# The first inverse stage on quarters of the array: symmetric halves instead of 49 full outputs, unfolded on VectorE

## The chip, the cores and the metric

The kernel runs on one core of one Trainium2 chip. The metric is the device time of one execution in microseconds (us), as the median of several runs. An execution is also profiled; the profile names the engines PE (TensorE products, PEld its weight loads), DVE (VectorE), ACT (ScalarE), POOL (GpSimd) and SP (SyncE, which here issues nearly all the DMAs).

## The reference

Two blocks over x of shape (8, 3136, 256): a frequency-domain block, then a Fourier mixing block with an MLP.

```
X  = rfft(x, axis=1);  Y = soft_threshold(X @ complex weights + bias, 0.01)
y  = irfft(Y, n=3136, axis=1)                  # block 1
u  = y + real(fft(fft(y, axis=1), axis=2))     # block 2
un = (u - mean(u)) / sqrt(var(u) + 1e-6)       # over the 256 columns
out = u + relu(un @ w_ch1) @ w_ch2             # 256 -> 1024 -> 256
```

All of it is float32. 3136 = 64 x 49, so a position is n = 49 n1 + n2 with n1 below 64 and n2 below 49, and a transform along the sequence is done in two stages.

## The kernel before

The eight sequences go through one after the other, in overlapping phases: the forward transform (p1, p2_f2), the products with the complex weights (p2_w), the mixing values (p2_mix), the inverse transform (p2_yt, p2_g2 and the start of p3_norm) and the MLP (p3_tr, p3_mlp1, p3_mlp2). Each phase of each sequence is a generator that yields a due time; the program resumes the earliest one, and what it then writes goes into the engines' queues. T is the due time of one sequence, some 215 us in the middle of the run. Each engine works its queue in order, so the code's due times set what stands behind what.

The frequencies of a sequence lie in 32 slots u of up to 50 values; a quarter q of the work holds 8 slots. The inverse transform has two stages.

- First stage, per slot: `p2_yt` transposes the spectrum Y (tile `y`) on PE into `g_yt`, two slots and 512 columns at a time (L908), and takes it out of PSUM. `p2_g2` multiplies it with a table `tif` (100 frequencies by 98 outputs: 49 values of n2 times two parts) into `g_g` (named g_g2 in the program), and DVE copies that to `bev` (L941), which goes to DRAM as `bd`. Sequence 0 does this in plain float32 with one product (L937). Sequences 1 to 7 split both operands into a high and a low fp32r part (ACT casts `yh`, `tih`, L919 and L900; DVE subtracts for `yl`, `til`, L157) and run three fp32r products through `mm3` (L163, L164, L165). Four steps i per quarter, two slots each: 16 steps per sequence.
- Second stage: `p3_norm` loads four pairs of n2 rows from `bd` as `bf` (`load_bf`, L974), multiplies them with `inv_f` over the slots, and DVE adds the mixing values `mt` (L1061). The products run on quarters of the array: `quads` cuts the 128 x 128 array into four 64 x 64 pieces with an operand each, `pair` takes two PSUM banks and has DVE clear one column of each as a mark (L370), and `run_quads` issues the products one behind the other (first L378, then L383). Six groups of 8 rows each per sequence, and a seventh for the last sequence that collects what is left over of all eight.

PSUM: all these tiles (`g_...`) rotate through the four banks of tag g; `h` and `o` of the MLP have two banks each. In the MLP, PE makes `h`, ACT and DVE turn it into `hh` and `hl` (L1109, L1110), and PE reads those for `o`.

The same cut into quarters is used by the second forward stage (`g_f<-tff,af`), and from sequence 3 on by the first one (`g_f<-xf,fwd_f`), where DVE first replaces the two halves of `xf` by sum and difference (L521, L522); each of those runs is put right behind a second-stage run of the inverse (`waiting`).

Of the kernel before, what the change touches and what calls it, by code (L numbers as in the profile page):

```python
# [55 lines left out]
def tables():  # L56
# [23 lines left out]
    for u in range(U):  # L80
# [14 lines left out]
        else:  # L95
# [8 lines left out]
            ti[1, :z, u, 1] = (co * sg).T / N  # L104
    p = np.arange(128)
# [10 lines left out]
        ti=ti.transpose(0, 1, 2, 4, 3).reshape(100, U, 98),  # L116
        cs=cs, mask=mask, ident=np.eye(128),
# [23 lines left out]
def spectral_block(ctx: ExitStack, tc: tile.TileContext, x, w_ri, b_ri, w1, w2,  # L141
                   c_fwd, c_fwd0, c_inv, c_tf, c_ti, c_cs, c_mask, c_ident, out):
# [69 lines left out]
    inv_f = cp.tile([128, 128], F32, name="inv_f")  # L212
    nc.sync.dma_start(out=fwd_0, in_=c_fwd0)
# [79 lines left out]
    lows = [cp.tile([100, 2, 128], F32, name=f"low{i}") for i in range(2)]  # L293
    for t in lows:
        va.memset(t[:, :, 0:1], 0.0)
# [40 lines left out]

    def n2_rows(t, n0, n):

        return t[n0:n0 + n].rearrange("n c u d -> (c u) n d")
# [367 lines left out]
    def p2_w(b):  # L707

        for q in range(4):
# [5 lines left out]
            y = sb.tile([128, 2, 8, 2, S], F32, tag="Y", bufs=2, name="Y")  # L715
# [58 lines left out]
    def p2_mix(b):  # L774
# [12 lines left out]
        for q in range(4):  # L787
# [4 lines left out]
            if b == 0:  # L792
                ef = sb.tile([128, 2, 8, S], F32, tag=("eh", "el")[q % 2], bufs=1, name="ef")
            else:
                eh = sb.tile([128, 2, 4, 100], F32R, tag="eh", bufs=1, name="eh")
                el = sb.tile([128, 2, 4, 100], F32R, tag="el", bufs=1, name="el")
# [78 lines left out]
    def p2_yt(b):  # L875

        for q in range(4):
# [6 lines left out]
            for i in range(4):  # L884
                yield base + STEP * (M0 + 0.022 + 0.185 * i)
                s = i // 2
                if i % 2 == 0:
                    if b == 1 and q == s == 0:
                        tif = tabs.pop((1, 0))
                    else:  # L890
                        tag = ("tif", "tih", "tif", "til")[(2 * q + s) % 4] if b == 0 else "tif"
                        tif = sb.tile([100, 4, 98], F32, tag=tag, bufs=2 if tag == "tif" else 1, name="tif")
                        behind("mt" if b == 1 else 3, out=tif, in_=c_ti[:, u0 + 4 * s:u0 + 4 * s + 4, :])
                    if b == 0:
                        tabs[b, q, s] = tif, None
                    else:
                        tih = sb.tile([100, 4, 98], F32R, tag="tih", bufs=1, name="tih")
                        til = sb.tile([100, 4, 98], F32R, tag="til", bufs=1, name="til")
                        with tc.issue_after(ends["t"][0]) if b == 1 and q == s == 0 else nullcontext():
                            sc.copy(tih, tif)  # L900
                        with tc.issue_after(ends["t"][1]) if b == 1 and q == s == 0 else nullcontext():
                            lo_v(til, tif, tih)
                        tabs[b, q, s] = tih, til
                gt = gtile("g_yt")
                for v in range(2):
                    place = 2 * (2 * (i % 2) + v) + s
                    for o in range(2):
                        te.transpose(gt[:100, (v * 2 + o) * 128:(v * 2 + o + 1) * 128],  # L908
                                     y[:, o, place].rearrange("p c j -> p (c j)"), ident)
                if b == 0:  # L910
# [4 lines left out]
                    yhl[b, q, i] = yf, None  # L915
                    continue
                yh = sb.tile([100, 512], F32R, tag="yh", bufs=2, name="yh")
                yl = sb.tile([100, 512], F32R, tag="yl", bufs=2, name="yl")
                sc.copy(yh, gt[:100])  # L919
                lo_v(yl, gt[:100], yh)  # L920
                yhl[b, q, i] = yh, yl

    def p2_g2(b):

        bd = b_dram[b] = dr.tile([N2, 2, U, D], F32, tag="bd", bufs=8, name=f"bd{b}")
        for q in range(4):
            base, STEP, F2W, W0, WW, M0 = clock2(b, q)
            for i in range(4):
                yield base + STEP * (M0 + 0.35 + 0.185 * i)
                tih, til = tabs[b, q, i // 2]  # L930
                yh, yl = yhl.pop((b, q, i))
                g = gtile("g_g2")
                for v in range(2):
                    cols = slice(v * D, v * D + D)
                    t = 2 * (i % 2) + v
                    if b == 0:
                        te.matmul(g[:98, cols], tih[:, t], yh[:, cols], start=True, stop=True)  # L937
                    else:
                        mm3(g[:98, cols], tih[:, t], til[:, t], yh[:, cols], yl[:, cols])
                bev = sb.tile([98, 512], F32, tag="ev" if b == 0 and q == 3 and i < 3 else "bev", bufs=3, name="bev")  # L940
                (va.tensor_copy if b else sc.copy)(bev, g[:98])  # L941
# [15 lines left out]
    def p3_norm(b):  # L957

        def load_bf(gi):

            g0, z = groups[b][gi]
            bf = sb.tile([128, 1024], F32, tag="b4", bufs=2, name="bf")
            for k in range(2):
                rows = bf[64 * k:64 * k + 64].rearrange("p (n d) -> p n d", d=D)
                if b == gi == 0:
                    with tc.issue_after(af_ld["md", 0, 3]):
                        af_ld["bf0"] = nc.sync.dma_start(out=rows, in_=b_dram[0][k:8:2].rearrange("n c u d -> (c u) n d")).ins
                    continue
                if g0 == 24:
                    for i in range(4):  # L970
                        nc.sync.dma_start(out=rows[:, i:i + 1], in_=n2_rows(b_dram[4 * k + i], N2 - 1, 1))
                    continue
                with tc.issue_after(af_ld["mt"]) if b == 0 and gi == 1 else nullcontext():
# [250 lines left out]
```

## Time and profile before

| | us |
|---|---|
| median of 3 runs (1818.59 to 1819.58) | 1819.08 |
| the profiled execution | 1818.19 |
| its span, first to last instruction | 1816.4 |

The profile is of one execution. Busy time counts from an instruction's start to its end; products on PE overlap, so the distance from one start to the next is what a product costs PE, and the duration beside it is longer. Instruction counts of PE in the profile are higher than in the program for plain float32, which runs in two passes.

### The profile page before, as it was taken

To read this page: it belongs to the slowest core of one execution; us is meant where nothing else is said; L and a number is where in the kernel's file an instruction comes from. 1 tells how busy PE (TensorE), PEld (TensorE's weight loads), DVE (VectorE), ACT (ScalarE), POOL (GpSimd) and SP (SyncE) were. 2 spreads that over 40 slices of the span, in tenths; PEclk is the share of its full clock that TensorE was granted. 3 is DMA by queue.
4 is the path that set the end of the run, shared out by engine and by line. 5 is a ranking of instruction groups with operands and counts; after the bars stand their busy time and mean duration, and the time that the engine had idled before them with its cause. 6 is when DMAs were issued, how large, how long until landed. Compare 5 with 4: busy or idle time off the path is not lost.

```text
span 1816.4 us, 39769 instructions
## 1 busy us (share of the span) xinstructions
PE 1789.0 (98%) x15258; PEld 1550.9 (85%) x15258; DVE 1221.2 (67%) x2890; ACT 821.3 (45%) x1754; POOL 329.5 (18%) x725
## 2 busy tenths in 40 slices
PE   8899999999999999999999999999999999999999
PEld 5677888888888888888888888888888889888888
DVE  4877777777667776767767766776666677654442
ACT  3774444444444444444444444544444444322221
POOL 1202222221122221112222112222111222010000
PEclk9999999999999999999999999999999999999999
DMA  7969553553536444355434535454232543152100
GB/s 215 264 213 245 151 157 123 142 148 95 147 104 171 120 130 130 111 148 164 130 94 130 158 103 149 128 159 119 90 106 84 145 113 90 48 138 68 50 13 35
DMA packets 169831, 232.98 MB, mean 128 GB/s; under 512 B 18434, under 2 KB 124936, under 8 KB 169641
## 3 DMA queue, kind: packets, MB, share of 16 engines
q1 hardware_dynamic: 167913, 228.87, 43.8%
q8 instruction: 120, 1.97, 0.5%
q10 hardware_dynamic: 1728, 1.57, 0.3%
q14 instruction: 70, 0.57, 0.1%
HBM read 126.04 MB, written 104.33 MB: 127 GB/s over the span
## 4 chain that ended last, share of the span: by engine, by line
PE 91%; DVE 5%; DMA 3%; ACT 1%; SPq 1%; issue 0%; DVEq 0%; ACTq 0%
PE o L163 10%; PE o L164 10%; PE o L165 10%; PE h L163 10%; PE h L165 10%; PE h L164 10%; PE g_f L383 4%; PE g_w L163 3%; PE g_w L165 3%; PE g_w L164 3%; PE g_yt L908 3%; PE g_g L378 3%; PE g_ut L1084 2%; PE g_g L163 1%; PE g_g L165 1%; PE g_mix L825 1%
## 5 line engine op out<-in xcount | busy, mean ns | idle before, releaser
L1110 DVE SCALAR_TENSOR_TENSOR hl<-h,hh 128x512 fp32r<-128x512 f32 x392 | 270.0, 689 | 362.9 <-ACT hh L1109 362.0
L164 PE MATMUL o<-w2h,hl 128*128 128x256 f32 x1568 | 431.7, 284 | 3.0 <-DVE hl L1110 2.9
L1109 ACT ACTIVATE hh<-h 128x512 fp32r<-128x512 f32 x392 | 234.4, 598 | 433.2 <-PE h L165 411.2
L165 PE MATMUL o<-w2h,hh 128*128 128x256 f32 x1568 | 422.6, 279 | 0.0
L163 PE MATMUL o<-w2l,hh 128*128 128x256 f32 x1568 | 402.4, 287 | 0.0
L163 PEld LDWEIGHTS o<-w2l,hh 128*128 128x128 f32 x1568 | 286.2, 188 | 42.9 <-issue 22.1
L163 PE MATMUL h<-utl,w1h 128*128 128x512 f32 x784 | 314.8, 401 | 0.0
L164 PE MATMUL h<-uth,w1l 128*128 128x512 f32 x784 | 311.8, 398 | 0.0
L165 PE MATMUL h<-uth,w1h 128*128 128x512 f32 x784 | 310.3, 396 | 0.0
L164 PEld LDWEIGHTS o<-w2h,hl 128*128 128x128 f32 x1568 | 295.1, 188 | 13.3 <-DVE hl L1110 6.6
L165 PEld LDWEIGHTS o<-w2h,hh 128*128 128x128 f32 x1568 | 295.5, 188 | 2.5 <-issue 0.2
L165 PEld LDWEIGHTS h<-uth,w1h 128*128 128x128 f32 x784 | 147.4, 188 | 32.3 <-issue 2.0
L163 PEld LDWEIGHTS h<-utl,w1h 128*128 128x128 f32 x784 | 147.5, 188 | 22.5 <-issue 4.5
L164 PEld LDWEIGHTS h<-uth,w1l 128*128 128x128 f32 x784 | 147.8, 188 | 18.1 <-issue 1.0
L1013 POOL TENSOR_SCALAR vv<-ag 128x2 f32<-128x2 f32 x98 | 19.4, 198 | 728.5 <-DVE ag L1010 705.3
L765 ACT ACTIVATE r<-g_w,two_t 128x400 f32<-128x400 f32 x128 | 76.2, 596 | 104.1 <-DVE g_w L761 93.6
L160 POOL TENSOR_TENSOR Xl<-xi,Xh 128x400 fp32r<-128x400 f32 (+1 forms) x61 | 64.6, 1061 | 204.0 <-ACT Xh L636 203.4
L761 DVE SCALAR_TENSOR_TENSOR g_w<-g_w,bias,ks 128x400 f32<-128x400 f32 x128 | 81.5, 637 | 27.0 <-PE g_w L165 25.8
L157 DVE TENSOR_TENSOR yl<-g_yt,yh 100x512 fp32r<-100x512 f32 x112 | 76.4, 684 | 26.4 <-ACT yh L919 26.0
L1135 DVE SCALAR_TENSOR_TENSOR ut<-o,rs,ut 128x256 f32<-128x256 f32 x196 | 83.0, 474 | 12.7 <-PE o L165 12.6
L908 PE MATMUL g_yt<-ident,Y 128*100 128x128 f32 x512 | 84.0, 273 | 4.7 <-DVE yl L157 2.1
L766 DVE SCALAR_TENSOR_TENSOR Y<-g_w,r 128x400 f32<-128x400 f32 x128 | 72.9, 570 | 21.5 <-ACT r L765 20.2
(169 smaller groups left out, 3327.9 us busy)
## 6 DMA issues: line engine op xcount, KB each, us to landing
bd<-bev SPq DMA_DIRECT2D x128, 196.0 KB
out_dram<-ut SPq DMA_DIRECT2D x98, 256.0 KB
bf<-bd SPq DMA_DIRECT2D x96, 256.0 KB
mt<-md SPq DMA_DIRECT2D x192, 128.0 KB
ad<-ev SPq DMA_DIRECT2D x91, 256.0 KB
af<-ad SPq DMA_DIRECT2D x112, 208.0 KB
md<-mq SPq DMA_DIRECT2D x112, 192.0 KB
tif<-c_ti SPq DMA_DIRECT2D x64, 153.1 KB
```

What stands on the lines that cost most here:

```text
L157: return va.tensor_sub(out_, full, hi.bitcast(F32))
L163: te.matmul(o, lh, rl, start=start, stop=False)
L164: te.matmul(o, ll, rh, start=False, stop=False)
L165: return te.matmul(o, lh, rh, start=False, stop=stop)
L383: mm = te.matmul(*o, start=True, stop=True)
L761: va.scalar_tensor_tensor(gw, gw, bias[:, c, o:o + 1], ks, op0=ALU.add, op1=ALU.add)
L765: ra = sc.activation(r, gw, AF.Relu, bias=lam_t)
L766: ya = va.scalar_tensor_tensor(y[:, o, :, c, :], gw, LAM, r, op0=ALU.add, op1=ALU.min)
L908: te.transpose(gt[:100, (v * 2 + o) * 128:(v * 2 + o + 1) * 128], y[:, o, place].rearrange("p c j -> p (c j)"), ident)
L1109: sc.activation(hh[:, :w], h[:, :w], AF.Relu)
L1110: dv = va.scalar_tensor_tensor(hl[:, :w], h[:, :w], 0.0, hh[:, :w].bitcast(F32), op0=ALU.max, op1=ALU.subtract)
L1135: va.scalar_tensor_tensor(ut[:, j], o[:, j * D:j * D + D], rs[:, j], ut[:, j], op0=ALU.mult, op1=ALU.add)
```

## The change

Sequences 1 to 7 only (sequence 0 keeps its stage and its table).

- The first stage gives, per slot and for the 25 values m of n2 from 0 to 24, the part that is even in n2 and the part that is odd, instead of 49 values of n2. With n2 = m and n2 = -m being sum and difference of the two, cosine and sine frequencies need not be mixed: the sum over 100 frequencies by 98 outputs becomes two sums over 50 frequencies by 52 outputs (25 m and one padding, times two parts). The table `c_tg` has 128 rows (two halves of 64) and 64 columns.
- `y` is padded so that a slot's two parts start 64 columns apart, POOL clears the padding, and the transposes take 128 columns instead of 100. ACT copies them to one float32 tile `yf`; there is no low part.
- `p2_g2` works on two steps at once: two banks and eight plain float32 products of 64 x 64 (50 by 52 used) with 256 columns, through `run_quads`. DVE copies both banks out; each goes to DRAM in two DMAs of 52 rows, where one of 98 rows stood per step.
- `bf` now has the two halves (even, odd) of four m; DVE makes sum and difference of them (two instructions per group) behind the last `hl`, 0.05 T ahead of the second stage, or 0.015 T for a sequence's first group, whose load is moved ahead by a fifth of a group. `inv_b` is a second table of the second stage.
- The rows of a group are m and -m instead of consecutive n2, so `mt` is loaded in another order (two of four loads now have contiguous 4 KB pieces), the last group collects n2 = 0, and the host puts the rows back accordingly.

```diff
@@ p2_w
-            y = sb.tile([128, 2, 8, 2, S], F32, tag="Y", bufs=2, name="Y")
+            yr = sb.tile([128, 16 * 114 + 14], F32, tag="Y", bufs=2, name="Y")
+            if b:
+                yr = yr[:, :]
+                y = bass.AP(yr.tensor, yr.offset, [yr.ap[0], (912, 2), (114, 8), (64, 2), (1, S)])
+                gp.memset(bass.AP(yr.tensor, yr.offset + S, [yr.ap[0], (114, 16), (1, 14)]), 0.0)
+                gp.memset(yr[:, 16 * 114:], 0.0)
...
@@ p2_yt
-                        tih = sb.tile([100, 4, 98], F32R, tag="tih", bufs=1, name="tih")
-                        til = sb.tile([100, 4, 98], F32R, tag="til", bufs=1, name="til")
...
+                            te.transpose(gv, bass.AP(yv.tensor, yv.offset, [yv.ap[0], (1, 128)]), ident)
...
-                yh = sb.tile([100, 512], F32R, tag="yh", bufs=2, name="yh")
-                yl = sb.tile([100, 512], F32R, tag="yl", bufs=2, name="yl")
-                sc.copy(yh, gt[:100])
-                lo_v(yl, gt[:100], yh)
-                yhl[b, q, i] = yh, yl
+                yf = sb.tile([128, 512], F32, tag=("yh", "yl")[i % 2], bufs=2, name="yf")
+                sc.copy(yf, gt)
+                yhl[b, q, i] = yf
@@ p2_g2
+                if b and i % 2 == 0:
+                    continue
...
+                if b:
+                    yfs = [yhl.pop((b, q, j)) for j in (i - 1, i)]
+                    gs, marks = pair("g_g2")
+                    ops = []
+                    for v, p, r in ((v, p, r) for v in range(2) for p in range(2) for r in range(2)):
+                        rows, cols = slice(64 * r, 64 * r + S), slice(v * D, v * D + D)
+                        ops.append((gs[r][64 * p:64 * p + 64, cols], tif[rows, 2 * p + v], yfs[p][rows, cols]))
+                    run_quads(ops, marks)
+                    for r, g in enumerate(gs):
+                        bev = sb.tile([128, 512], F32, tag="bev", bufs=3, name="bev")
+                        va.tensor_copy(bev, g)
+                        for p in range(2):
+                            u = 8 * q + 2 * (i - 1 + p)
+                            st_eng.dma_start(out=bd[r][:, :, u:u + 2].rearrange(...), in_=bev[64 * p:64 * p + 52])
+                    continue
...
-                        mm3(g[:98, cols], tih[:, t], til[:, t], yh[:, cols], yl[:, cols])
@@ p3_norm
+                if b:
+                    yield t0 + T3 * (NRM - 0.2)
+                    yield from after(("b", b))
+                    nxt = load_bf(0)
                 yield t0 + T3 * NRM
                 yield from after(("b", b), ("m", b))
-                if b:
-                    nxt = load_bf(0)
                 mt = load_mt(g0, z)
+            if b and g0 < 24:
+                yield g1_time(b, gi) - (FOLD if gi else 0.015) * T
+                e, o = nxt[:, 0:512], nxt[:, 512:]
+                with tc.issue_after(last_hl[0]):
+                    va.tensor_add(e, e, o)
+                va.scalar_tensor_tensor(o, o, -2.0, e, op0=ALU.mult, op1=ALU.add)
...
-            run_quads(quads(gs, lambda rows, cols: inv_f[rows, rows], bf.rearrange("q (i p d) -> q p i d", p=2, d=D)), marks, (b, gi))
+            run_quads(quads(gs, lambda rows, cols: inv_b[rows] if b and g0 < 24 and cols.start else inv_f[rows, rows],
+                            bf.rearrange("q (p i d) -> q p i d", p=2, d=D)), marks, (b, gi))
```

PE's queue in the middle of the run, before: one step of the first inverse stage behind products of the MLP. The number behind g_g is the buffer's; the three products stand a second time for the second slot.

```order
L164 MATMUL o<-w2h,hl 128x256
L165 MATMUL o<-w2h,hh 128x256
L163 MATMUL o<-w2l,hh 128x256
L163 MATMUL g_g_13208<-yl,tih 98x256
L164 MATMUL g_g_13208<-yh,til 98x256
L165 MATMUL g_g_13208<-yh,tih 98x256
```

The same stage after the change, a pair of steps, every tile with its buffer number: two banks (g_g2), two transposed tiles (yf), one table (tif). The four products stand a second time for the second slots.

```order
L190 MATMUL g_w_11822<-Xh_11263,wsl_288 128x400
L191 MATMUL g_w_11822<-Xh_11263,wsh_287 128x400
L399 MATMUL g_g2_11845<-yf_11504,tif_11497 64x256
L404 MATMUL g_g2_11846<-yf_11504,tif_11497 64x256
L404 MATMUL g_g2_11845<-yf_11663,tif_11497 64x256
L404 MATMUL g_g2_11846<-yf_11663,tif_11497 64x256
```

Twelve full-array products in two places became eight products on quarters in one place, 56 times in all.

DVE's queue ahead of a second-stage run that also carries a forward run, before: the sum and difference of `xf`, with `hl` of the MLP around them.

```order
L1110 SCALAR_TENSOR_TENSOR hl<-h,hh 128x512
L521 TENSOR_TENSOR xf<-xf 128x512
L1110 SCALAR_TENSOR_TENSOR hl<-h,hh 128x512
L522 SCALAR_TENSOR_TENSOR xf<-xf 128x512
L157 TENSOR_TENSOR yl<-g_yt,yh 100x512
L370 MEMSET g_f_7802 128x1
```

The same place after the change:

```order
L1169 SCALAR_TENSOR_TENSOR hl<-h,hh 128x512
L542 TENSOR_TENSOR xf<-xf 128x512
L543 SCALAR_TENSOR_TENSOR xf<-xf 128x512
L666 TENSOR_TENSOR xs<-g_f_7547,xi 128x400
L391 MEMSET g_f_7668 128x1
L391 MEMSET g_f_7669 128x1
L391 MEMSET g_f_7723 128x1
L1169 SCALAR_TENSOR_TENSOR hl<-h,hh 128x512
L1094 TENSOR_TENSOR bf<-bf 128x512
L391 MEMSET g_f_7724 128x1
L1095 SCALAR_TENSOR_TENSOR bf<-bf 128x512
L1169 SCALAR_TENSOR_TENSOR hl<-h,hh 128x512
```

The sum and difference of `bf` now stand between the same `hl` instructions, and `yl` is gone.

## Rows read from the trace of the kernel before

**Rows 1.** The page: each engine's busy time, share of the span, instructions.
```profile
PE 1789.0 (98%) x15258; PEld 1550.9 (85%) x15258; DVE 1221.2 (67%) x2890; ACT 821.3 (45%) x1754; POOL 329.5 (18%) x725
```

**Rows 2.** The page: the chain that ended last, shares by engine.
```profile
PE 91%; DVE 5%; DMA 3%; ACT 1%; SPq 1%; issue 0%; DVEq 0%; ACTq 0%
```

**Rows 3.** Windows of one steady period: length, busy us (instructions) by engine, clock, DMA share.
```profile
836.00:1050.00 214.00, 213.36 (x1887) 186.90 (x1885) 150.91 (x360) 100.34 (x213) 42.27 (x90) 1.00 0.45 131
```

**Rows 4.** Waits of PE: who, for whom, us in total, times, longest.
```profile
PE o L164 <- DVE hl L1110: 2.9, 9, 0.3
```

**Rows 5.** Groups by line and form: what is removed (`busy us, mean ns | idle before`).
```profile
L163 PE MATMUL g_g<-yl,tih 100*98 100x256 f32 x224 | 64.6, 289 | 0.0
L157 DVE TENSOR_TENSOR yl<-g_yt,yh 100x512 fp32r<-100x512 f32 x112 | 76.4, 684 | 26.4 <-ACT yh L919 26.0
L157 DVE TENSOR_TENSOR til<-tif,tih 100x392 fp32r<-100x392 f32 x56 | 31.5, 562 | 0.5 <-ACT tih L900 0.5
L900 ACT CAST tih<-tif 100x392 fp32r<-100x392 f32 x56 | 29.2, 521 | 57.1 <-PE g_g L165 55.4 <-DMA ad<-ev 1.2
```

**Rows 6.** Timeline of PE, 925 to 927 us: start, duration, instruction.
```profile
925.36 0.28 PE L163 MATMUL g_g<-yl,tih 100*98 100x256 f32 x1
...
926.07 0.35 PE L163 MATMUL g_w<-Xl,wdh 128*128 128x400 f32 x1
```

**Rows 7.** Timeline of PE, 1426 to 1428.6 us: one run on quarters of the array.
```profile
1426.15 0.39 PE L164 MATMUL h<-uth,w1l 128*128 128x512 f32 x1
1426.38 0.40 PE L165 MATMUL h<-uth,w1h 128*128 128x512 f32 x1
1426.70 0.64 PE L378 MATMUL g_g<-bf,inv_f 64*64 64x512 f32 x1
1426.71 0.65 PE L383 MATMUL g_g<-bf,inv_f 64*64 64x512 f32 x3
1427.18 0.59 PE L378 MATMUL g_g<-bf,inv_f 64*64 64x512 f32 x1
1427.19 0.60 PE L383 MATMUL g_g<-bf,inv_f 64*64 64x512 f32 x3
1427.72 0.50 PE L163 MATMUL o<-w2l,hh 128*128 128x256 f32 x2
1428.07 0.28 PE L164 MATMUL o<-w2h,hl 128*128 128x256 f32 x1
```

**Rows 8.** Groups by line and form: weight loads of the two kinds of transposes.
```profile
L908 PEld LDWEIGHTS g_yt<-ident,Y 128*100 128x100 f32 x512 | 57.8, 127 | 16.0 <-DVE yl L157 3.2 <-DVE Y L766 1.9 <-DVE mq L835 1.2
L1084 PEld LDWEIGHTS g_ut<-ident,ut 128*128 128x128 f32 x392 | 48.2, 141 | 9.1
```

**Rows 9.** Timeline of PE, 904.3 to 905.2 us: a product behind transposes.
```profile
904.47 0.27 PE L908 MATMUL g_yt<-ident,Y 128*100 128x128 f32 x1
904.50 0.43 PE L163 MATMUL g_w<-Xsl,wrh 128*128 128x400 f32 x1
904.76 0.34 PE L164 MATMUL g_w<-Xsh,wrl 128*128 128x400 f32 x1
904.95 0.34 PE L165 MATMUL g_w<-Xsh,wrh 128*128 128x400 f32 x1
```

**Rows 10.** Groups by line and form on DVE: nearest rows for what is added.
```profile
L941 DVE COPY bev<-g_g 98x512 f32<-98x512 f32 x112 | 76.7, 685 | 15.8 <-PE g_g L165 14.3
L521 DVE TENSOR_TENSOR xf<-xf 128x512 f32<-128x512 f32 x31 | 26.0, 838 | 0.0
L522 DVE SCALAR_TENSOR_TENSOR xf<-xf 128x512 f32<-128x512 f32 x31 | 21.2, 684 | 0.4
L370 DVE MEMSET g_g<- 128x1 f32 x96 | 5.2, 59 | 5.0 <-ACT xr L649 3.0 <-ACT ks L742 0.3
```

**Rows 11.** Timeline: issue of a sequence's first bf loads, and the stage that reads it.
```profile
979.02 2.58 SPq L974 DMA_DIRECT2D bf<-bd  x4
...
996.56 0.64 PE L378 MATMUL g_g<-bf,inv_f 64*64 64x512 f32 x1
```

More of the change, by code (lines that the diff above doesn't have):

```diff
@@ L104, in tables @@
             ti[1, :z, u, 1] = (co * sg).T / N
+    tg = np.zeros((2, 64, U, 2, 32))
+    for u in range(U):
+        t, sg = slot_freqs(u)
+        ph = 2 * np.pi * (np.outer(t, m) % N) / N
+        co, si = np.cos(ph) / N, np.sin(ph) / N
+        if u == 0:
+            for c in range(2):
+                j = np.arange(25 * c, 25 * c + 25)
+                w = np.full((25, 1), 2.0)
+                w[0 if c == 0 else 24] = 1.0
+                tg[0, j, 0, c, :NM] = co[j] * w
+                tg[1, j, 0, c, :NM] = -si[j] * w
+        else:
+            z, sg = len(t), sg[:, None]
+            tg[0, :z, u, 0, :NM] = co
+            tg[0, :z, u, 1, :NM] = si
+            tg[1, :z, u, 0, :NM] = -si * sg
+            tg[1, :z, u, 1, :NM] = co * sg
+    ib = np.zeros((2, U, 2, 32))
+    ib[0, 0] = 1.0
+    ib[1, 0] = np.where((n1h + 1) % 2, -1.0, 1.0)
+    for u in range(1, U):
+        phh = 2 * np.pi * (((n1h + 1) * u) % N1) / N1
+        ib[0, u] = 2 * np.cos(phh)
+        ib[1, u] = 2 * np.sin(phh)
     p = np.arange(128)
@@ L212, in spectral_block @@
     inv_f = cp.tile([128, 128], F32, name="inv_f")
+    inv_b = cp.tile([128, 64], F32, name="inv_b")
     nc.sync.dma_start(out=fwd_0, in_=c_fwd0)
@@ L291, in keep_busy @@
                 last = te.matmul(o, mean_m, m, start=True, stop=True).ins
-    lows = [cp.tile([100, 2, 128], F32, name=f"low{i}") for i in range(2)]
-    for t in lows:
-        va.memset(t[:, :, 0:1], 0.0)
+    lows = []
     two_t = cp.tile([128, 2], F32, name="two_t")
@@ L335, in after @@
             yield now[0] + 10
-    def n2_rows(t, n0, n):
-        return t[n0:n0 + n].rearrange("n c u d -> (c u) n d")
     def a_rows(t, m, n):
@@ L794, in p2_mix @@
             else:
+                for i in range(2 * (b == 1 and q == 0)):
+                    lows.append(sb.tile([100, 2, 128], F32, tag=("tih", "til")[i], bufs=1, name="low"))
+                    gp.memset(lows[i][:, :, 0:1], 0.0)
                 eh = sb.tile([128, 2, 4, 100], F32R, tag="eh", bufs=1, name="eh")
@@ L891, in p2_yt @@
                         tag = ("tif", "tih", "tif", "til")[(2 * q + s) % 4] if b == 0 else "tif"
[L892 to L896, printed above, removed]
-                        tih = sb.tile([100, 4, 98], F32R, tag="tih", bufs=1, name="tih")
-                        til = sb.tile([100, 4, 98], F32R, tag="til", bufs=1, name="til")
[L899 to L903, printed above, removed]
+                        tif = sb.tile([128, 4, 64] if b else [100, 4, 98], F32, tag=tag, bufs=2 if tag == "tif" else 1, name="tif")
+                        behind("mt" if b == 1 else 3, out=tif, in_=(c_tg if b else c_ti)[:, u0 + 4 * s:u0 + 4 * s + 4, :])
+                    tabs[b, q, s] = tif
+                    if b == 1 and q == s == 0:
+                        behind("mt", out=inv_b, in_=c_invb)
                 gt = gtile("g_yt")
@@ L934, in p2_g2 @@
                     cols = slice(v * D, v * D + D)
[L935 to L938, printed above, removed]
-                        mm3(g[:98, cols], tih[:, t], til[:, t], yh[:, cols], yl[:, cols])
-                bev = sb.tile([98, 512], F32, tag="ev" if b == 0 and q == 3 and i < 3 else "bev", bufs=3, name="bev")
-                (va.tensor_copy if b else sc.copy)(bev, g[:98])
+                    te.matmul(g[:98, cols], tif[:, 2 * (i % 2) + v], yf[:, cols], start=True, stop=True)
+                bev = sb.tile([98, 512], F32, tag="ev" if q == 3 and i < 3 else "bev", bufs=3, name="bev")
+                sc.copy(bev, g[:98])
                 u = 8 * q + 2 * i
```

73 lines of the change are left out of this document (46 added, 27 removed).

## The prediction

> **What bounds the kernel now.** I read the engines' busy shares first. PE is busy 98% of the span, its weight loads 85%, DVE 67%, ACT 45%, POOL 18% [rows 1]. As products overlap, a busy PE need not be a bound, so the chain of waits comes second: 91% of what ended last is PE itself, 5% DVE, 3% DMA [rows 2]. Third, a steady period of 214 us: PE busy 213.4 of them at a granted clock of 1.00 (the upper level, 2.4 GHz), DVE 151, DMA share 0.45 [rows 3]. Last, the waits of PE: for the engine nearest to it, DVE with `hl`, it waits 2.9 us in the whole run [rows 4]. So from about 200 us on the time is the sum of what the products cost PE from start to start, and the change is worth what it takes from that sum, as long as no wait of the same size appears. DVE, ACT and POOL matter only as possible late suppliers.
>
> **The change on PE.** Removed: in sequences 1 to 7 the three fp32r products of a slot. There are 224 of each of the three kinds [rows 5], 672 in all, twelve for each of the 56 pairs of steps that the new code works on at once. Their durations, about 0.29 us each, overlap; the cost is the distance of the starts. Six of them stand from 925.36 to 926.07, 0.71 us [rows 6], so a pair costs 1.42 us, and 56 pairs 79.5 us.
>
> Added: eight plain float32 products per pair, on quarters, with 256 columns each: two per quarter, 512 columns per quarter. A run of the second stage has four such products with 512 columns, one per quarter, which is the same number of columns per quarter in the same two passes. Such a run, alone, is in the rows: the last `h` product starts at 1426.38 and would cost 0.23 us (1426.15 to 1426.38); the first pass of the four quarters starts at 1426.70 and 1426.71, so they do run at once; the second pass at 1427.18, 0.48 us on; the first `o` product starts at 1427.72, and the third at 1428.07, where two of 0.12 us (0.71 / 6 [rows 6]) would take 0.24 [rows 7]. The run takes the place of 1428.07 - 1426.38 - 0.23 - 0.24 = 1.22 us. Of that 0.09 us is the entry (0.32 against 0.23), 0.11 us the slow first product behind it, and the rest the two passes with the way out. With 1.22 us a pair, 56 pairs cost 68.3 us. The program's order has only 55 more runs on quarters than before (109 become 164), since one pair stands right behind a second-stage run; that saves one entry and exit, under 0.4 us. PE: 68.0 - 79.5 = -11.5 us.
>
> The bounds of the new run: below, four passes of half the length with no entry or exit, twice 0.48 us, 0.96 us or 53.8 us in all (-25.7). Above, each of the two extra rounds inside the run costs an entry again, 0.09 us: 1.40 us, 78.4 us in all (-1.1). I take 1.22, since the row has the same shape and number of columns.
>
> What speaks against quarters is the change of shape, 1.22 us where the two passes alone are 0.96. The Trainium skill, TensorEngine Tiling (Array Packing), Key Properties, says that changing the tiling mode, not merely the tile, drains the engine; its table of theoretical speedups counts the tiles alone. By the table without the drain the sum would be the lower bound, -26 us; by the row, which has the drain in it, it is -11.5. The row decides.
>
> Transposes: the stationary side grows from 100 to 128 columns, the moving side stays at 128 columns. Their weight loads take 127 ns, those of the transposes with 128 columns 141 ns [rows 8]; if the 14 ns counted, 448 times would be 6 us. I take nothing, since a weight load runs beside the product before it (85% and 98% busy at once [rows 1]), and keep the 6 us for the range. A full product behind transposes starts its successor late: 904.50 to 904.76 is 0.26 us where the next takes 0.19 [rows 9], 0.07 us lost. The order has 216 such places where it had 233: -1.2 us.
>
> Sum on PE: -11.5 - 1.2 = -12.7 us.
>
> **The change on DVE, ACT and POOL.** All of it lies beside PE's work. DVE loses 112 `yl` of 684 ns and 56 `til` of 562 ns [rows 5], 76.4 + 31.5 = 107.9 us. It gains 42 sums and 42 differences of `bf`; the same two instructions on `xf` take 838 and 684 ns [rows 10], so 42 x 1.52 = 63.9 us; and 112 marks of 59 ns, 6.6 us. The copies of `bev` stay 112 and go from 98 to 128 partitions, which the width per partition doesn't change (685 ns [rows 10]). DVE: -37 us of 1221. ACT loses 56 casts of 521 ns [rows 5], -29 us, and the 112 casts become copies. POOL gains 56 clearings of up to 224 columns, which no row shows; at the mean of POOL's instructions, 329.5 / 725 = 0.45 us [rows 1], that is 25 us, at a bound of three times that 76 us, on an engine that is idle 82% of the time. None of this is in the sum: PE does not wait for these engines now [rows 4]. What it costs if that cover goes is in the first two rivals.
>
> The added waits. The sum of `bf` waits for its load at the head of DVE's queue, and `hl` stands behind it, then PE's `o`. A sequence's first loads are issued from 979.02 on, 2.6 us of issuing, and read by PE at 996.56 [rows 11], 15 us later; the load is moved ahead by a fifth of a group (some 7 us) and the sum stands 0.015 T (3 us) ahead of the products, so the margin grows. The later groups' loads are issued a group or more ahead. I take nothing. The pair's marks wait for two of four banks, also on DVE; again nothing is taken. SP issues 221 DMAs more (1414 become 1635); at 0.65 us each (2.58 for four [rows 11]) 144 us at most, spread over the span, with mean DMA share 0.45.
>
> **The time.** The profiled execution took 1818.19 us (span 1816.4), 0.9 below the median. 1819.08 - 12.7 = 1806.4 us.
>
> **The rivals.**
> - Banks and marks (no change, or nearly). A pair holds two banks until DVE has copied both, 2 x 0.685 = 1.37 us [rows 10], where a step held one. The next products find two banks; the six of a `g_w` take 1.14 us at 0.19 [rows 9]. If a third user of a bank follows at once, PE waits 1.37 - 1.14 = 0.23 us per pair, 12.9 us in all; then the time is 1819. Where products of `o` and `h` stand behind the pair nothing is lost, as those have banks of their own; with a quarter of the loss gone it is 1816, which I take. For it: four banks serve everything but the MLP. Against: more than half of the pairs in the order have `o` or `h` behind them. The Trainium skill, TensorEngine Tiling (Array Packing), PSUM Bottleneck, states this: tiles make the products faster and not the way out of PSUM. The trace agrees so far as the copy, 0.685 us, is longer than a product; no row shows PE waiting for it.
> - DVE's sums in front of `hl` (slower). Six times per sequence 1.52 us more stand between two `hl`, in up to 31 cases beside the 1.52 us of `xf` that are there now, with two `bev` copies that now come together. Were one instruction of each, 0.684 us, to end up in front of a product that needs `hl`, that is 42 x 0.684 = 28.7 us, and the time 1835. It decides from 12.7 / 42 = 0.30 us per group on. For it: DVE works in order and is busy 151 of 214 us. Against: the 31 sums of `xf` have the same place, and PE's waits for `hl` are 2.9 us for all 392 of them; in exchange 2.7 `yl` and 1.3 `til` per group are gone.
> - A cheaper run (faster than forecast): the entry hides behind weights loaded ahead, 0.96 us a pair: 1819.08 - 25.7 - 1.2 = 1792.
> - The quarters don't run at once, since two products of a round share a table but not the moving tile. Then a pair costs four times its passes, 3.8 us, and the time is 1819 + 56 x 2.4 = 1953. Against: the four of [rows 7] start 10 ns apart, and their moving sides differ as well.
>
> **How the numbers follow.** Forecast 0.70, banks 0.13, DVE 0.08, cheaper run 0.07, not at once 0.02. The forecast's own range, from the bounds of the run and small waits, is 1799 to 1814. For 8 in 10 the range goes to 1797 on one side (half of the cheaper run) and to 1816 on the other (the bank rival's value); left out are DVE, not-at-once, half of the cheaper run and a third of the banks, together 0.18. Two tenths of a per cent are 3.6 us, about what this kernel's runs can tell from nothing. Faster: forecast 0.70, cheaper run 0.07, a third of the banks 0.05, in all 0.82. Same: 0.08 of the banks. Slower: 0.10.
>
> **What would show it.** In the profile after: the three fp32r kinds of `g_g` gone and a run of the new products taking 1.2 us from the product before to the third behind, in the timeline; PE's busy time down by about 12 us with its share still 98%; DVE at about 1184 us and ACT at about 792; PE's waits for `hl` still a few us. The forecast is wrong if the new run lasts over 1.4 us, if PE's waits for `hl`, for a mark or for a bank add up to 10 us, or if `bf` sums have long idle time in front of them that a DMA ends.

## The result and the profile after

The changed kernel takes 1801.72 us (median of 4 runs, 1799.97 to 1802.88) where the kernel before takes 1819.33 beside it (4 runs, 1818.59 to 1820.06): the ratio is 0.990, 95% interval 0.9884 to 0.9916, or 17.6 us less. The forecast was 1806.4, with 12.7 us less; the time is inside the range. The profiled execution took 1802.17 us.

The engines' busy times in the profile after, the answer to [rows 1]:

```profile
PE 1776.4 (99%) x15482; PEld 1503.3 (84%) x15482; DVE 1167.4 (65%) x2916; ACT 788.0 (44%) x1698; POOL 334.9 (19%) x783
```

And the chain that ended last, by engine, the answer to [rows 2]:

```profile
PE 94%; DMA 3%; DVE 1%; ACT 1%; issue 1%; SPq 1%; DVEq 0%; ACTq 0%
```

PE is still the bound, and more so: 94% of the chain where it was 91%, DVE 1% where it was 5%. A steady period, from one product to the same product one sequence later (an `o` that is the first to read its `hl`), took 214.80 us before and takes 212.12 now, at the same clock, and PE is busy for all of it; the window of [rows 3] was laid at 214 us by hand and is no period (window: length, busy us by engine, clock, DMA share; before, then after):

```profile
841.96:1056.76 214.80, 214.14 (x1891) 187.49 (x1889) 151.71 (x360) 101.03 (x216) 42.27 (x90) 1.00 0.45 130
832.35:1044.47 212.12, 212.12 (x1921) 181.05 (x1920) 142.00 (x365) 95.95 (x207) 43.33 (x99) 1.00 0.44 132
```

The new run stands alone at 1339 us (timeline of PE: start, duration, instruction; each float32 product shows as two passes, so 16 rows for eight products):

```profile
1339.53 0.39 PE L191 MATMUL h<-uth,w1h 128*128 128x512 f32 x1
1339.85 0.43 PE L399 MATMUL g_g<-yf,tif 50*64 50x256 f32 x1
1339.86 0.44 PE L404 MATMUL g_g<-yf,tif 50*64 50x256 f32 x3
1340.12 0.38 PE L399 MATMUL g_g<-yf,tif 50*64 50x256 f32 x1
1340.13 0.82 PE L404 MATMUL g_g<-yf,tif 50*64 50x256 f32 x11
1340.88 0.45 PE L189 MATMUL g_w<-Xl,wdh 128*128 128x400 f32 x1
1341.16 0.34 PE L190 MATMUL g_w<-Xh,wdl 128*128 128x400 f32 x1
1341.34 0.34 PE L191 MATMUL g_w<-Xh,wdh 128*128 128x400 f32 x1
```

It is read as [rows 7] were: the `h` product would cost 0.23 us, two `g_w` products 0.18 each, and from 1339.53 to the third product are 1.81, so the run takes the place of 1.81 - 0.23 - 0.36 = 1.22 us. Counted in the same way, the 51 runs of this kind that stand between full products take 1.20 us at least and 1.22 in the median.

Of PE's waits, the row of [rows 4] has no successor: the view after names no wait of `o` for `hl` at all. But the view counts such a wait only from the modelled end of the product before it. Counted from start to start (an `o` product that begins 55 ns after the end of the `hl` it reads, and later than its usual distance behind the product before), PE lost 7.1 us at 16 places before, and 1.3 us at 7 after. This is how one of nine places of 0.565 us looked before (DVE, then PE):

```profile
931.46 0.15 DVE L835 TENSOR_TENSOR mq<-g_mix,mq 100x1 f32<-100x1 f32 x1
931.52 0.75 DVE L837 TENSOR_TENSOR mq<-mq 100x256 f32<-100x256 f32 x2
932.19 0.68 DVE L1110 SCALAR_TENSOR_TENSOR hl<-h,hh 128x512 fp32r<-128x512 f32 x1
```

```profile
932.11 0.49 PE L908 MATMUL g_yt<-ident,Y 128*100 128x128 f32 x3
932.93 0.38 PE L164 MATMUL o<-w2h,hl 128*128 128x256 f32 x1 [0.32 <-DVE hl L1110]
```

The last `h` product that this `hl` needs began at 929.70. With DVE free, `hl` begins 1.06 us behind that; here DVE is busy with `Y`, `eo` and `mq` until 2.5 us behind it, and `o` stands until 932.93. What puts `mq` there is the order of PE's products. The last `g_mix` product of the quarter, from which `mq` is made, stands 2.21 us in front of that `h` product:

```profile
927.49 0.23 PE L827 MATMUL g_mix<-cs,el 128*100 128x128 f32 x1
929.70 0.39 PE L165 MATMUL h<-uth,w1h 128*128 128x512 f32 x1
```

After, the same `g_mix` product stands 1.95 us behind the `h` product that this `hl` needs; `hl` begins 1.13 us behind that `h` product, and `o` 2.80 us behind it without a wait:

```profile
919.75 0.40 PE L191 MATMUL h<-uth,w1h 128*128 128x512 f32 x1
920.88 0.69 DVE L1169 SCALAR_TENSOR_TENSOR hl<-h,hh 128x512 fp32r<-128x512 f32 x1 [0.23 <-ACT hh L1168]
921.70 0.22 PE L858 MATMUL g_mix<-cs,el 128*100 128x128 f32 x1
922.55 0.28 PE L190 MATMUL o<-w2h,hl 128*128 128x256 f32 x1
```

The distances are the same at all nine places, in both profiles. PE's own work between `h` and `o` is about the same (2.67 us before without the wait, 2.80 after): it is `hl` that comes earlier. `mq` now precedes a later `hl`, which waits for ACT, not for DVE, and no product of PE is late for it:

```profile
925.34 0.75 DVE L868 TENSOR_TENSOR mq<-mq 100x256 f32<-100x256 f32 x2
926.49 0.69 DVE L1169 SCALAR_TENSOR_TENSOR hl<-h,hh 128x512 fp32r<-128x512 f32 x1 [0.34 <-ACT hh L1168]
```

PE's starts, added up over the stretch that holds all changed products (1641.5 us before, 1623.9 after), give the account: the 672 removed products cost 81.6 us; 55 runs of 1.22 and one behind another run of 0.88 cost 68.0; so -13.6. The waits for `hl` give -5.8. The sum is -19.4, and +1.8 is left that I have not assigned. (The spans of these two executions differ by 16.0 us, not 17.6, as what lies outside the stretch took 1.6 us longer after.)

### The profile page after: what moved, and what is told of

The parts are those of the page before. It is cut to its first block, busy times and chain, and to the rows that moved or that the text cites. A ratio compares the mean times of both kernels' runs of the same rounds, so it can differ in the third digit from the quotient of the medians.

```text
span 1800.4 us, 40505 instructions
## 1 busy us (share of the span) xinstructions
PE 1776.4 (99%) x15482; PEld 1503.3 (84%) x15482; DVE 1167.4 (65%) x2916; ACT 788.0 (44%) x1698; POOL 334.9 (19%) x783
## 4 chain that ended last, share of the span: by engine, by line
PE 94%; DMA 3%; DVE 1%; ACT 1%; issue 1%; SPq 1%; DVEq 0%; ACTq 0%
PE o L189 11%; PE o L190 10%; PE h L189 10%; PE h L190 10%; PE h L191 10%; PE o L191 10%; PE g_g L399 4%; PE g_f L404 4%; PE g_w L189 4%; PE g_w L191 4%; PE g_w L190 4%; PE g_yt L937 3%; PE g_ut L1143 2%; PE g_mix L856 2%; PE g_g L404 2%; PE g_f L563 1%
## 5 line engine op out<-in xcount | busy, mean ns | idle before, releaser
L189 PE MATMUL o<-w2l,hh 128*128 128x256 f32 x1568 | 412.8, 289 | 0.0
L789 DVE SCALAR_TENSOR_TENSOR g_w<-g_w,bias,ks 128x400 f32<-128x400 f32 x128 | 81.6, 637 | 27.1 <-PE g_w L191 25.8
L870 POOL TENSOR_TENSOR mq<-mq 100x508 f32<-100x508 f32 x28 | 37.5, 1339 | 328.7 <-DVE mq L868 202.1
L183 DVE TENSOR_TENSOR utl<-g_ut,uth 128x512 fp32r<-128x512 f32 x98 | 66.6, 686 | 24.5 <-ACT uth L1145 24.1
```

The lines of the kernel that those rows point to most:

```text
L183: return va.tensor_sub(out_, full, hi.bitcast(F32))
L189: te.matmul(o, lh, rl, start=start, stop=False)
L789: va.scalar_tensor_tensor(gw, gw, bias[:, c, o:o + 1], ks, op0=ALU.add, op1=ALU.add)
```

## The experiments

The open question was where the 5 us beyond the forecast come from. Theory T1: from the order of the program, which puts `hl` and the product that reads it at other places. T2: from the relief of DVE, which no longer forms `yl` and `til`. The other experiments price the rivals. Each time is a median, each ratio is against the kernel before on the same chip; after stands at 0.9900. Wherever an instruction is added or taken away, the program's order moves a little on every engine, PE too; where an expectation says that PE's order is kept, it was wrong in that.

**Before without the low parts**

```diff
-                            lo_v(til, tif, tih)
-                        tabs[b, q, s] = tih, til
+                        tabs[b, q, s] = tih, tih
...
-                lo_v(yl, gt[:100], yh)
-                yhl[b, q, i] = yh, yl
+                yhl[b, q, i] = yh, yh
```

> The kernel before, without the two kinds of VectorE subtractions (112 yl, 56 til; 108 us of VectorE); the third product of a slot reads the rounded tables again in the place of the low parts, so the low part of the products is left out of the computation. PE's products and their order are those of before. After lost 17.6 us where my sum had 12.7, and PE's starts say that about 5.8 us of it are waits of `o` for `hl` that went. Theory T1 (order: these waits go because in the new program order more of PE's work stands between a last `h` product and the product that needs `hl`): the time of before, 1819 +- 1.5, the waits still about 7 us in 16 places. Rival T2 (relief: they go because VectorE no longer has yl and til in front of `hl`): about 1813 to 1814, and the waits go to 1 or 2 us.

1820.44 us, ratio 0.9999 (0.9989 to 1.0008): no gain, though DVE is busy 1127 us instead of 1221. The nine waits of 0.565 us are gone, ten of 0.29 us stand there (six of them where before had one, four new; 3.1 us in all at 12 places), and PE waits elsewhere instead:

```profile
PE g_yt L907 <- ACT yh L917: 6.1, 9, 0.7
```

At the nine places `hl` comes as late as before, 2.48 us behind its `h` product and behind `mq`. PE only stands earlier, at the transposes in front of `o`:

```profile
926.31 0.39 PE L165 MATMUL h<-uth,w1h 128*128 128x512 f32 x1
928.12 0.75 DVE L837 TENSOR_TENSOR mq<-mq 100x256 f32<-100x256 f32 x2
928.78 0.68 DVE L1107 SCALAR_TENSOR_TENSOR hl<-h,hh 128x512 fp32r<-128x512 f32 x1
929.89 0.53 PE L907 MATMUL g_yt<-ident,Y 128*100 128x128 f32 x3 [0.68 <-ACT yh L917]
```

The time is as T1 said; the waits are between the two. Taking `yl` and `til` away from before is not worth 5 us, and does not bring these `hl` forward.

**After with DVE's load put back, all of it**

```diff
                     tabs[b, q, s] = tif
+                    if b: va.tensor_tensor(tif, tif, tif, op=ALU.max)
...
                 sc.copy(yf, gt)
+                va.tensor_sub(gt, gt, yf)
```

> The kernel after, with VectorE's load of before put back as work that changes nothing: a subtraction of 128 x 512 into the bank of the transposes behind every copy `yf`, and a maximum of each table with itself (about 108 us in all, more than before had). PE's products and their order are those of after. T1 (order): the time of after, 1801.7 +- 1.5. T2 (relief): 1806 to 1808, with PE waiting for `hl` again in about 16 places. My rival 'sums in front of hl' would also show here, as VectorE is now fuller than it was before: up to 1817.

1836.66 us, ratio 1.0084 (1.0062 to 1.0106), by the ratios some 34 us above after; neither theory's number. DVE's waits point to a cause: its instruction on a table stands at the head of the queue until the table's load has landed.

```profile
DVE tif L926 <- DMA tif<-c_tg: 77.6, 37, 5.3
```

So what was added was not only work (102 us of instructions) but waiting of a kind that before's `til` did not have (0.5 us [rows 5]). The run says nothing about T1 and T2.

**After with the subtractions alone put back**

```diff
                 sc.copy(yf, gt)
+                va.tensor_sub(gt, gt, yf)
```

> The kernel after with the subtractions alone put back (112 of about 0.68 us, 77 us of VectorE, on the bank of the transposes behind each copy `yf`; they change nothing in the numbers). The earlier run with more put back took 35 us, but there the instruction on a table waited for the table's load at the head of VectorE's queue, 78 us in all, which before's `til` did not. If the waiting for the load was the cause: 1802 to 1806. If VectorE simply has no room for sums and subtractions at once (T2): 1812 to 1835.

1806.69 us, ratio 0.9926 (0.9913 to 0.9938), by the ratios 4.7 us above after, with 77 us of instructions more on DVE (its busy time is 66 us longer). PE's waits for `hl` are 4.3 us at 9 places. That is just above the band for the load as the cause of the 34 us, so most of those came with the instruction on the table: 77.6 us of waits and 24 us of work, which no run takes apart. And 5 us are what T2 gave in the expectation before, so such work has a cost in the new kernel. But none of the 9 places is one of before's nine: there PE's order is that of after in eight cases, `hl` begins at most 1.41 us behind its `h` product in those, and no `o` waits.

```profile
925.34 0.40 PE L191 MATMUL h<-uth,w1h 128*128 128x512 f32 x1
926.46 0.69 DVE L1170 SCALAR_TENSOR_TENSOR hl<-h,hh 128x512 fp32r<-128x512 f32 x1 [0.23 <-ACT hh L1169]
```

**After without the folding**

```diff
-                with tc.issue_after(last_hl[0]):
-                    va.tensor_add(e, e, o)
-                va.scalar_tensor_tensor(o, o, -2.0, e, op0=ALU.mult, op1=ALU.add)
```

> The kernel after, without the two VectorE instructions that form sum and difference of `bf` in sequences 1 to 7 (42 groups x 1.52 us); the folding is left out of the computation, everything on PE stays. T1: the fold costs nothing, 1801.7, at most 1.5 less. Rival (VectorE's sums stand in front of `hl`; it decides at 0.30 us a group): 13 us less or more, 1789; a part of it would be in between.

1800.89 us, ratio 0.9887 (0.9873 to 0.9901), 1 to 2 us below after, with intervals that overlap. The sums of `bf` cost nothing that can be told.

**After with the folding three times**

```diff
-                with tc.issue_after(last_hl[0]):
-                    va.tensor_add(e, e, o)
-                va.scalar_tensor_tensor(o, o, -2.0, e, op0=ALU.mult, op1=ALU.add)
+                for _ in range(3):
+                    with tc.issue_after(last_hl[0]):
+                        va.tensor_add(e, e, o)
+                    va.scalar_tensor_tensor(o, o, -2.0, e, op0=ALU.mult, op1=ALU.add)
```

> The kernel after, with sum and difference of `bf` formed three times over (84 x 1.52 us = 128 us more on VectorE, in one piece of 4.6 us in front of each group; the numbers computed are others). It prices the rival of the sums in front of `hl`: if a sum there were on the path, 42 x 3.04 us = 128 us would be added, 1929. T1: VectorE has room (65% busy), 0 to +3 us, 1802 to 1805, most likely a few waits for `hl` or for the first product that reads `bf`.

1839.25 us, ratio 1.0101 (1.0088 to 1.0114), 37 us above after; T1 expected 0 to 3. PE's waits, 24 of the 37 us:

```profile
PE o L189 <- ACT hh L1169: 13.3, 9, 1.9
PE g_f L399 <- DVE g_f L391: 5.9, 8, 1.6
PE o L190 <- DVE hl L1170: 5.0, 10, 1.8
```

Sum and difference once, 1.5 us per group, fit into the gaps of DVE; three times, 4.6 us in one piece, do not. The mechanism of the rival exists, though `hh`, which ACT makes, is late for longer than `hl`; what holds ACT up is not shown.

**Before with `mq` behind `hl`**

```diff
+            if b: yield base + STEP * (M0 + 0.372 + 0.394 * 1.5 + 0.03)
             for i, f in ((0, va.tensor_add), (1, va.tensor_sub)):
-                f(even[:, :, i::2], even[:, :, i::2], odd[:, :, 0:1].to_broadcast((100, 4, 64)))
+                with tc.issue_after(last_hl[0]) if b and last_hl[0] is not None else nullcontext():
+                    f(even[:, :, i::2], even[:, :, i::2], odd[:, :, 0:1].to_broadcast((100, 4, 64)))
```

> The kernel before, in which the last two wide `mq` instructions of a quarter on VectorE stand behind the next `hl` instead of in front of it, in sequences 1 to 7; everything else, PE's order too, is as before. In the trace of before, PE waits 0.565 us at nine places because `hl` begins only when these two end (2.49 us behind the start of the last `h` product, where 1.06 would do), and at seven others 0.29 us with VectorE free. Theory T1, sharpened (place: five of the 17.6 us went because the new order puts `hl` in front of `mq`): 9 x 0.565 = 5.1 us less, 1814 to 1815, with the seven waits of 0.29 us left. Rival T2 (relief: they went because VectorE lost yl and til): some other VectorE work delays `hl` in its place, 1818 to 1819. Third theory (no part of the gain lies in these waits, as PE catches up later): 1819 to 1820 with the waits gone.

1825.99 us, ratio 1.0032 (1.002 to 1.0044): 6 us slower. The nine waits are gone, but DVE is late with the next `hl` instructions, and PE's row for `hl` is longer than in [rows 4]:

```profile
PE o L164 <- DVE hl L1113: 5.4, 18, 0.4
```

From start to start it is 11.6 us at 33 places. T1 in the form "this one place" falls.

**Before with the copies `bev` on ACT**

```diff
-                (va.tensor_copy if b else sc.copy)(bev, g[:98])
+                sc.copy(bev, g[:98])
```

> The kernel before, with the 112 copies `bev` of sequences 1 to 7 on ScalarE instead of VectorE (77 us off VectorE, some 67 us more on ScalarE, which is busy 44%); yl and til stay. With the subtractions put back after lost about 5 us, and moving `mq` behind `hl` in before only moved the waits on, so theory T2 (relief: what went with yl and til are waits of PE on a VectorE that is full for stretches of 5 to 10 us) stands. By T2 any 77 us off VectorE do in before what yl did: 1814 to 1816, PE's nine waits of 0.565 us gone. If it is yl and til themselves, or the order: 1820 +- 1.5.

1824.63 us, ratio 1.0022 (1.0012 to 1.0031): with 71 us less on DVE (1149.9) the kernel is 4 us slower. The place of the nine waits is still there, with 1.04 instead of 0.565 us each; `mq` and `Y` stand in front of `hl` as before, and now later:

```profile
936.70 0.57 DVE L766 SCALAR_TENSOR_TENSOR Y<-g_w,r 128x400 f32<-128x400 f32 x1
937.19 0.14 DVE L835 TENSOR_TENSOR mq<-g_mix,mq 100x1 f32<-100x1 f32 x1
937.25 0.75 DVE L837 TENSOR_TENSOR mq<-mq 100x256 f32<-100x256 f32 x2
937.92 0.68 DVE L1110 SCALAR_TENSOR_TENSOR hl<-h,hh 128x512 fp32r<-128x512 f32 x1
```

ACT, which got the copies, is not what is late here: `hh` begins at 935.38, lasts 0.60 us, and `hl` follows 1.9 us behind its end. T2 falls as a rule: DVE's total does not set these waits.

**Before with the mix written later**

```diff
-                yield base + STEP * (M0 + 0.372 + 0.394 * ui / 2)
+                yield base + STEP * (M0 + 0.41 + 0.394 * ui / 2)
```

> The kernel before with one number of the order changed: the products `g_mix` of a quarter are written 0.41 instead of 0.372 of a step behind their time (2 us later); no instruction is added or removed. In its order the last `mq` instruction stands directly in front of `hl` on VectorE at 4 places instead of 19. Relief has fallen as a cause (77 us off VectorE made before 4 us slower, its nine waits growing from 0.565 to 1.04 us). If the order alone makes the 5 us by which after beat the sum of its products: some other time than 1820, and with these nine waits gone 1814 to 1816. If the new waits that come are as large, as they were when `mq` alone was moved: 1820 to 1826. If the time doesn't depend on such places at all: 1820 +- 1.5.

1823.29 us, ratio 1.0022 (1.0011 to 1.0032). No instruction differs, only the order: 4 us slower. At the nine places the last `g_mix` product now stands 0.99 us behind the `h` product, `hl` begins 1.88 us behind it instead of 2.49, and the waits are gone. In their place five of before's seven waits of 0.29 us have grown to 0.61, and four of 0.45 are new: 5.2 us at 10 places in all. The order alone makes and takes away such waits, so T1 holds in this weak form; a better order of before was not found.

**After with one of two copies `bev` on ACT**

```diff
-                        va.tensor_copy(bev, g)
+                        (sc.copy if r else va.tensor_copy)(bev, g)
```

> The kernel after, with one of the two copies `bev` of every pair on ScalarE (38 us off VectorE; both banks are free after 0.69 us instead of 1.37). By T2 little is left to win, as without the folding the time fell by only 0.8 us: 1801 to 1802. If the banks of a pair held PE up somewhere: 1798 or less. If ScalarE is late now with `hh`: 1804 or more.

1804.22 us, ratio 0.9913 (0.99 to 0.9927), by the ratios 2.4 us above after, not told apart with certainty; waits for `hl` 4.7 us at 9 places. That is in the band which the expectation gave to a late `hh`, but PE's waits name none for `hh`. No gain from freeing a pair's banks earlier shows.

**After with narrower transposes**

```diff
-                            te.transpose(gv, bass.AP(yv.tensor, yv.offset, [yv.ap[0], (1, 128)]), ident)
+                            te.transpose(gv[:114], bass.AP(yv.tensor, yv.offset, [yv.ap[0], (1, 114)]), ident)
...
-                sc.copy(yf, gt)
+                sc.copy(yf[:114], gt[:114])
```

> The kernel after with transposes of 114 instead of 128 columns (the 14 columns left out are zeros between the halves' tables that only some products read with weight zero). My term for the wider transposes was nothing, with 6 us kept for the range: 448 x 14 ns. If the width counts like that, the time falls by 6 us; if not, it stays, 1801.7 +- 1.5.

1802.71 us, ratio 0.9897 (0.9882 to 0.9911): no gain. The weight loads take 134 ns instead of 140, so at most 2.7 us were at stake, not the 6 of the expectation. The traces before and after say more: the 448 transposes of sequences 1 to 7 cost 39.6 us from start to start with 100 columns (without the nine waits behind them) and 39.5 with 128. The width costs nothing.

**After with runs merged**

```diff
@@ run_quads
+        elif pending and not own:
+            k = next(iter(pending))
+            more, m = pending.pop(k)()
             ops, marks = ops + more, marks + m
...
@@ p2_g2
-                    run_quads(ops, marks)
...
+                    until = now[0] + 0.36 * STEP
+                    if not (q == i == 3):
+                        pending[b, q, i] = post
+                        while (b, q, i) in pending and now[0] < until:
+                            yield now[0] + 10
+                    if not gs:
+                        pending.pop((b, q, i), None)
+                        run_quads(*post(), own=True)
```

> The kernel after, in which a pair's products on quarters are held back for up to 0.36 of a step, and put directly behind the next run on quarters if one comes; 25 runs fewer (164 become 139), the same products. My run of 1.22 us has about 0.36 us at its edges (way in 0.09, way out 0.15 to 0.2, slow first product behind 0.11). If that is right: 25 x 0.36 = 9 us less, 1792 to 1793, as long as no wait appears. Rival (banks: the two runs in one need all four banks of TensorE's other work at once, and VectorE must empty them at 0.685 us each): the saving is eaten, 1800 to 1806, with PE waiting for marks or `g_f` copies. Rival (edges cost nothing, the price is in the two passes): 1801.7.

(`post` takes the pair's banks and returns its products.) 1811.9 us, ratio 0.995 (0.9939 to 0.9961), 9 us above after. The edge is as priced. A merged run in PE's timeline:

```profile
447.43 0.28 PE L189 MATMUL o<-w2l,hh 128*128 128x256 f32 x1
447.63 0.26 PE L405 MATMUL g_f<-tff,af 52*64 52x50 f32 x1
...
448.61 1.06 PE L410 MATMUL g_g<-yf,tif 50*64 50x256 f32 x16
449.59 0.39 PE L190 MATMUL o<-w2h,hl 128*128 128x256 f32 x1
449.82 0.28 PE L191 MATMUL o<-w2h,hh 128*128 128x256 f32 x1
449.93 0.28 PE L190 MATMUL o<-w2h,hl 128*128 128x256 f32 x1
```

From 447.43 to 449.93 less three `o` products of 0.115 us it is 2.16 us (median of 20: 2.17), where the two runs alone take 1.28 and 1.22: 0.33 us saved each time, 8.6 for the 26 merges. But a run of two pairs needs all four banks, and PE stands in front of other runs until DVE has marked theirs:

```profile
830.05 0.28 PE L189 MATMUL o<-w2l,hh 128*128 128x256 f32 x1
831.83 0.23 PE L405 MATMUL g_f<-tff,af 52*64 52x50 f32 x1 [1.51 <-DVE g_f L391]
```

Over the run (waits of PE) these are 5.6 us (after: 1.6); the waits for `hl` are 8.6 us from start to start (after: 1.3), of which 3.9 are one wait, at 298 us.

```profile
PE g_f L405 <- DVE g_f L391: 5.6, 6, 1.5
```

So some 11 of the 18 us between saving and loss are seen. The mechanism of the bank rival, which did not show for the change itself, is here, as a part of the loss; its time, 1800 to 1806, was too low.

**The same with one of two copies `bev` on ACT**

```diff
-                        va.tensor_copy(bev, g)
+                        (sc.copy if r else va.tensor_copy)(bev, g)
```

> The merged runs of the run before (26 merges, each 0.33 to 0.35 us cheaper by its trace, 9 us in all, and some 19 us of new waits for banks and `hl`), with one of a pair's two copies `bev` on ScalarE, so that the banks come free sooner. If the new waits come from the copies of the pair: a good part of the 10 us comes back, 1800 to 1804. If they come from the second stage's own long eviction, which now finds all four banks taken: 1810 to 1812.

1807.23 us, ratio 0.9931 (0.9918 to 0.9943): between a third and a half of the loss comes back (3.5 us by the ratios, whose intervals overlap, 4.7 by the medians), against expectations of most of it or nothing. PE waits longer for marks, 9.2 us:

```profile
PE g_f L405 <- DVE g_f L391: 9.2, 9, 2.4
```

So the pair's copies may be a part of the loss; a new order of the queues could give as much, and what the rest is stays open. No version was faster than after by more than the measurement tells.

## Why the prediction was right, point by point

The sign, the mechanism and the price of the new run are right; the gain is 4.9 us larger than forecast, mostly by waits that I had taken as too small to matter and that a new order of the queues took away.

| step | forecast | measured |
|---|---|---|
| removed products | 79.5 us | 81.6 (by all 672 starts) |
| added runs | 1.22 us each, 68.0 | 1.22, 68.0 |
| wider transposes | 0, at most +6 | 0 (39.6 us before, 39.5 after) |
| places behind transposes | -1.2 | 0 |
| waits of PE for `hl` | a few us, unchanged | 7.1, now 1.3 |
| DVE, ACT, POOL busy | -37, -29, +25 | -54, -33, +5 |

- The added run: the row of another stage with the same number of columns per quarter priced it to 0.01 us. Its edges were argued from that row; the merged kernel shows them, 0.33 us for one edge less. The run without edges (0.96 us) and the run with more of them (1.40) did not occur.
- The removed products: six starts in [rows 6] gave 0.118 us a product, all 672 give 0.121. The step was mis-sized by 2.1 us because one place stood for 56.
- The term of -1.2 us for full products behind transposes is not real: such a product starts 0.03 us behind the last transpose [rows 9], where others stand 0.11 apart, and that early start makes up for the late successor.
- "DVE, ACT and POOL matter only as possible late suppliers" was right for the forecast's sign, but the step "for `hl` PE waits 2.9 us in the whole run" [rows 4] read the wait too small: from start to start it was 7.1, and 5.8 of it went. For 5.1 of these, the nine places of 0.565 us, the cause is the order of the program: `g_mix` moved behind the `h` product, and `mq` with it. It is not the relief of DVE. Without `yl` and `til`, in before's order, `hl` is as late there as ever (2.48 us behind `h`); with 77 us put back, in after's order, none of the nine waits returns; and before with `g_mix` later loses them too. It is not more work of PE in between either, as T1 was first put. For the other 0.7 us, at the seven places of 0.29 us, the cause is open. Nor is such a gain one to count on: each edit of the queues makes other waits. Before got no faster by less work on DVE (1820.4 and 1824.6), by moving `mq` alone (1826.0) or by moving `g_mix` (1823.3). That the change drew an order with 5.8 us less of them was luck, as far as the forecast goes.
- DVE beside it: its busy time fell by 17 us more than forecast. 14 of these are `eo`, which reads the padded `Y` and takes 548 ns where it took 668; why is open. POOL's clearings take 11 us instead of 25. Neither is in the sum. The sums of `bf` have no idle time in front of them (0.3 us in all), as taken.
- The rivals: waits for the banks and marks of a pair do not show in the profile after, but do for the merged runs. DVE's sums in front of `hl` cost nothing at 1.5 us a group (within 2 us) and 37 us at 4.6. The quarters run at once: first passes at 1339.85 and 1339.86.
- The Trainium skill, TensorEngine Tiling (Array Packing), Key Properties, says that a change of tiling mode drains the engine. The traces agree so far as a run that shares its way in and out saves 0.33 us; how much of that is the drain is not taken apart.

## What to carry to other kernels

A run of small products on parts of the array was priced to 0.01 us here from another run in the trace with the same columns per part, taken from the product before it to the third behind it, edges included. What is removed should be summed over all its starts, not read at one place. In an engine-bound kernel, read waits from start to start, as the wait view hides what lies under the modelled end of the product before. And leave a few us of uncertainty for any edit: it reorders the queues of the other engines, and that alone moved this kernel by 4 and 6 us in two runs. When an edit gains or loses a few us too much, look for which product moved past which in PE's queue, before blaming the load of another engine.

## What the runs showed of the hardware

- A run on quarters costs 0.33 us at its edges, and it can be had back by putting two runs together: 2.17 us for 1.28 and 1.22 alone. The kernel that did so was slower all the same, with 5.6 us of waits for the marks of its banks.
- The stationary width of a transpose (100, 114 or 128 columns) did not show in the time, though its weight load does take longer: 140 ns for 128 columns, 127 for 100 (groups after, weight loads: busy us, mean ns).

```profile
L937 PEld LDWEIGHTS g_yt<-ident,Y 128*128 128x128 f32 x448 | 54.0, 140 | 11.6 <-ACT yf L946 2.0 <-POOL vv L1067 0.8
L935 PEld LDWEIGHTS g_yt<-ident,Y 128*100 128x100 f32 x64 | 6.9, 127 | 5.9 <-DVE Y L794 2.1 <-DVE mq L866 1.2 <-ACT ks L770 1.1
```

- On DVE, 71 to 94 us less busy time made the kernel before no faster. In the changed one, 66 us more in pieces of 0.7 us cost 5 us, and 126 us more in pieces of 4.6 us cost 37. What stands in front of an `hl` at a given place decided nine waits that the sum did not.
